# Down projection of chunks 0 and 1 as one Strassen pair, with q, k, v of two chunks in turn and a later exponential

## The chip, the cores and the metric

The kernel runs on one core of a Trainium2 chip. The metric is the device time of one execution in microseconds (us). Before the change it is 777.04 us, the median of three runs (776.59 to 777.09). Times in the text are us from the start of the profiled span unless something else is said.

## The reference

The input `x` has 2048 tokens of 1024 bf16 values. The kernel computes a layer norm, sliding-window attention with a residual, a second layer norm and a bilinear feed-forward part with a residual:

```
h   = x + attention(layernorm(x) @ wqkv) @ wo       # wqkv 1024 x 3072, wo 1024 x 1024
g   = layernorm(h) @ w_gate ;  u = layernorm(h) @ w_up      # 1024 x 3584 each
out = h + (g * u) @ w_down                                  # 3584 x 1024
```

Attention has 32 heads of 32 values. Token s looks at the eight tokens s, s-2, ..., s-14 of its head, with a softmax over the eight logits; positions before the first token are masked.

## The kernel before, in words

**Tiling.** The tokens are cut into four chunks of 512 (`TC`). A product with a weight runs on the tensor array in groups of eight matmuls of 128x128 by 512 columns (`mm_group`, L409), one for each 128 of the 1024 input values. Each group fills one of eight PSUM tiles ("mm"), which another engine has to copy out before it can be used again. For q, k, v there are six weight blocks of 512 columns per chunk and four groups per block (`qkv`, L414). ScalarE copies each group out (`evac_qkv`, L322: a copy of 512 columns, and for k and v two small copies of the 16 columns that the next chunk needs), and SyncE stores it to DRAM.

**Layer norm 1.** Its rows must be transposed before the array can use them. For chunk 3 ScalarE computes sums and squares (`NormOnScalar.sums`, L259) and the four normalized row tiles (`rows`, L277). Each tile of 128 tokens is then transposed by a DMA that SyncE issues (`transpose`, L225) into `lnT`. A q, k, v group reads all four of them.

**Attention.** `attention(c)` (L444) is a generator that mostly emits VectorE work: products of q with shifted k (L451), sums over the head (L453 to L461), the maximum (L466 to L470), an exponential on ScalarE (L471), sums and a reciprocal (L474 to L479), weights times shifted v (L494 to L504). Its operands qD, kD, vD are gathered from DRAM by loads that GpSimd issues (`load_qk` L428, `load_v` L435). The output goes to DRAM (L506) and comes back transposed as four quarters of `oT` (L509), for the output projection.

**Order of the work.** The program is written as one stream of instructions, and each engine runs its part of it in order. `Background` (L37) mixes the generators into the main loops. After each group the main loop calls `bg.step(1.73)`, which adds that time to a credit, times a rate, with a cap of 4.0; while the credit is positive, the next generator that is ready runs until its next `yield`, whose value is taken from the credit. A `yield "later", t` sets the generator aside for t us of the main loop's clock.

The main order is: q, k, v of chunks 0 and 1 (blocks partly in turn); all six blocks of chunk 2 (L765); blocks 0 to 3 of chunk 3; the output projection with layer norm 2 of chunk 0 (`wo_ln2`, L519); blocks 4 and 5 of chunk 3; gate and up of chunk 0 (`ffn1`, L602); `wo_ln2` of chunk 1; the plain down projection of chunk 0 (`ffn2`, L640, 224 matmuls at L646); gate and up of chunk 1; and then the down projection of chunk 1 alone by Strassen's scheme in Winograd's form.

**Strassen.** A product of two-by-two blocks is done with seven block products in place of eight, for additions of blocks on VectorE. Chunk 1's seven products are `dprod` (L805), each 2 x 14 = 28 matmuls, 196 in all, between the output projections of chunks 2 and 3 (`wo_adds`, L846). The operands are f16 and scaled by powers of two. The scales come from sums of absolute values, which ScalarE computes with its activation function (`abs_sum` L585, `abs_sum_down` L590, `abs_sum_h1` L598). Chunks 2 and 3 do gate and up, and then down, as a Strassen pair (`pair_block` L703; the down stage from L1053): there the two chunks are the two rows of blocks.

**Weights.** A list (`stream`, L129 to L157) fixes the order in which SyncE loads weight tiles into seven slots. `retire` frees slots and `pump` (L161) starts the next loads. Normalized rows and the outputs of the absolute sums that nobody reads ("junk") share a pool `ln` of four slots (L101).

Of the kernel before, what the change touches and what calls it, by code (L numbers as in the profile page):

```python
# [36 lines left out]
class Background:  # L37
# [15 lines left out]
    def step(self, us):  # L53
        self.now += us
        self.credit = min(self.credit + us * self.rate, 4.0)
# [23 lines left out]
def kernel(  # L79
# [41 lines left out]

    bg = Background()
# [13 lines left out]
    def stream_wd(c, hf):  # L136
        for b in range(4):
            stream.append((("wd", c, hf, b), wd_v[:, bass.ts(b, 7), bass.ts(hf, 512)], 7))

    NH = NF // 4  # L140
    for c in range(2):
        stream_wo(c)
        if c > 0:
            stream_wd(0, 0)
            stream_wd(0, 1)
        for b in range(7):
            stream.append((("wg", c, b), wg_v[:, :, bass.ts(b, 512)], KO))
            stream.append((("wu", c, b), wu_v[:, :, bass.ts(b, 512)], KO))
    def stream_down(name, e, hf, halves):
        for a in halves:  # L150
            stream.append((("dn", name, a), wd_e[e][:, bass.ts(a, 7), bass.ts(hf, 512)], 7))

    stream_down("21", 1, 0, (0, 1))
    stream_down("11", 0, 0, (0, 1))
    stream_wo(2)
    stream_down("12", 0, 1, (0,))
# [100 lines left out]
    class NormOnScalar(Norm1):  # L257

        def sums(self):  # L259
            room = small.tile([128, 4, 4], F32, tag="nroom", name=f"nroom{self.c}")  # L260
            self.s, self.nm, self.ss, self.nb = (room[:, i, :] for i in range(4))
            junk = lnp.tile([128, D], BF, tag="ln", name=f"njunk{self.c}")
            xs = xtiles[self.c]
            for t in range(4):
                nc.scalar.activation(junk[:], xs[t][:], ACTF.Copy, accum_out=self.s[:, t:t + 1])
                yield "later", GROUP_US
            nc.scalar.activation(self.nm, self.s, ACTF.Copy, scale=-1.0 / D)
            for t in range(4):
                nc.scalar.activation(junk[:], xs[t][:], ACTF.Square, bias=self.nm[:, t:t + 1],
                                     accum_out=self.ss[:, t:t + 1])  # L270
                yield "later", GROUP_US
# [4 lines left out]

        def rows(self):  # L277
            for t in range(4):
                ln = lnp.tile([128, D], BF, tag="ln", name=f"ln{self.c}_{t}")
                nc.scalar.activation(ln[:], xtiles[self.c][t][:], ACTF.Identity, bias=self.nb[:, t:t + 1],  # L280
                                     scale=self.rs4[:, t:t + 1])
                self.lns[t] = ln
                self.transpose(t)
                yield "later", GROUP_US
# [158 lines left out]

    def attention(c):  # L444
        qD, kD = qkv_in["q", c], qkv_in["k", c]
        lg = att.tile([128, W, SUB], F32, tag="lg", name=f"lg{c}")
        for wp in range(W // 2):
# [14 lines left out]
            yield 1.0  # L462
        if c == 0:
            nc.vector.tensor_tensor(lg[0:32, :, 0:16], lg[0:32, :, 0:16], mask[:], ALU.add)
# [5 lines left out]
        nc.vector.tensor_tensor(lg[:], lg[:], mx[:, None, :].to_broadcast((128, W, SUB)), ALU.subtract)  # L470
        nc.scalar.activation(lg[:], lg[:], ACTF.Exp, scale=float(DH) ** -0.5)  # L471
# [38 lines left out]
        oTs[c] = oT  # L510
        while c + 1 < NCH and ("q", c + 1) not in qkv_in:
# [7 lines left out]
    def wo_ln2(c):  # L519
# [8 lines left out]
        for t in range(4):  # L528
            for hf in range(2):
# [12 lines left out]
                bg.spend(0.7)  # L542
                bg.step(GROUP_US)
        norm(3)
        retire(2)
        return lnT, hs
# [35 lines left out]
    scale_gu, scale_d, scale_h = Scale("gu", 56), Scale("d", 56), Scale("h", 56)  # L582
    scale_h1 = Scale("h1", 28)

    def abs_sum(c, b, j):  # L585
        wt = wts["wg" if c == 0 else "wu", c, b]
        junk = lnp.tile([128, 2, 512], BF, tag="ln", name=f"junk{c}_{b}_{j}")
        scale_gu.add(28 * c + 4 * b + j, wt[:, bass.ts(j, 2), :], junk[:])

    def abs_sum_down(hf, b, j):  # L590
        junk = lnp.tile([128, 512], BF, tag="ln", name=f"junkd{hf}_{b}_{j}")
        scale_d.add(28 * hf + 7 * b + j, wts["wd", 0, hf, b][:, j, :], junk[:])
# [5 lines left out]
    def abs_sum_h1(f, ht):  # L598
        junk = lnp.tile([128, TC], BF, tag="ln", name=f"junke{f}")
        scale_h1.add(f, ht[:], junk[:])  # L600

    def ffn1(c, lnT, at={}):  # L602
        hT = []
        for b in range(7):
            if b == 5 and c + 1 < NCH:
                hss[c + 1] = load_x(c + 1, "h", nc.sync)
            for j in range(4):
                pg = psum.tile([128, TC], F32, tag="mm", name=f"pg{c}_{b}_{j}")
                mm_group(pg, wts["wg", c, b], j, lnT)
                gs = t1k.tile([128, TC], BF, tag="t1k", name=f"gs{c}_{b}_{j}")  # L610
                nc.scalar.copy(gs[:], pg[:])  # L611
                bg.step(GROUP_US)
                pu = psum.tile([128, TC], F32, tag="mm", name=f"pu{c}_{b}_{j}")
                mm_group(pu, wts["wu", c, b], j, lnT)
                us = t1k.tile([128, TC], BF, tag="t1k", name=f"us{c}_{b}_{j}")
                nc.scalar.copy(us[:], pu[:])  # L616
                nc.vector.tensor_tensor(gs[:], gs[:], us[:], ALU.mult)  # L617
                abs_sum(c, b, j)
                bg.spend(0.45)
                bg.step(GROUP_US)  # L620
                hT.append(gs)
                if (b, j) in at:
                    at[b, j]()
                f = len(hT) - 3
# [533 lines left out]
```

## Time and profile before

| what | value |
|---|---|
| median of 3 runs | 777.04 us (776.59 to 777.09) |
| profiled execution | 777.01 us, of which the span is 775.2 us |
| tensor array (PE) | 769.3 us busy, 3691 matmuls and transposes |
| VectorE | 605.3 us busy |
| ScalarE | 484.0 us busy |
| GpSimd | 142.1 us busy |
| DMA | 134.38 MB, mean 173 GB/s |
| granted clock of the array | full speed in all 40 slices |

| stage | from (us) | to (us) | matmul groups |
|---|---|---|---|
| plain down projection of chunk 0 | 301.7 | 350.0 | 224 matmuls |
| chunk 1's Strassen, output projections of 2 and 3 | 446.6 | 516.8 | 196 of Strassen and 128 |
| pair of chunks 2 and 3, gate and up | 516.8 | 687.0 | |
| pair of chunks 2 and 3, down | 687.0 | 775.2 | |

How to read a group line of the profile: it names the source line, the engine, the operation, output and inputs, the shape and the count; then the busy time in us with the mean of one in ns, and the idle time of the engine just before these instructions, with what ended most of it. A matmul's duration of 379 ns overlaps with the next one; the pitch of the array is the busy time divided by the count. In a timeline line the first number is the start and the second the duration; an issue on a queue (SPq is SyncE's, ACTq ScalarE's) lasts while the queue hands out the transfer, and a bracket gives how long the engine had been idle and what released it.

### The profile page before, as it was taken

To read this page: it belongs to the slowest core of one execution; us is meant where nothing else is said; L and a number is where in the kernel's file an instruction comes from. 1 tells how busy PE (TensorE), PEld (TensorE's weight loads), DVE (VectorE), ACT (ScalarE), POOL (GpSimd) and SP (SyncE) were. 2 spreads that over 40 slices of the span, in tenths; PEclk is the share of its full clock that TensorE was granted. 3 is DMA by queue.
4 is the path that set the end of the run, shared out by engine and by line. 5 is a ranking of instruction groups with operands and counts; after the bars stand their busy time and mean duration, and the time that the engine had idled before them with its cause. 6 is when DMAs were issued, how large, how long until landed. Compare 5 with 4: busy or idle time off the path is not lost.

```text
span 775.2 us, 10420 instructions
## 1 busy us (share of the span) xinstructions
PE 769.3 (99%) x3691; PEld 353.5 (46%) x3691; DVE 605.3 (78%) x766; ACT 484.0 (62%) x1040; POOL 142.1 (18%) x152
## 2 busy tenths in 40 slices
PE   8999999999999999999999999999999999999998
PEld 6444444444444444444444444444444444444444
DVE  5639999999999989999979859985553444578863
ACT  4639564322866662965777899746677776788240
POOL 0000000200002000011000001008778687600000
PEclk9999999999999999999999999999999999999999
DMA  8998896997947964978445592644332423740001
GB/s 278 265 260 199 157 230 151 299 271 224 310 133 236 308 235 125 288 257 277 142 143 192 182 299 68 157 98 114 109 95 69 109 59 106 240 140 28 0 28 55
DMA packets 183716, 134.38 MB, mean 173 GB/s; under 512 B 81264, under 2 KB 176496, under 8 KB 181616
## 3 DMA queue, kind: packets, MB, share of 16 engines
q1 hardware_dynamic: 176912, 110.12, 50.9%
q0 software_dynamic: 3584, 22.02, 8.9%
q10 hardware_dynamic: 3168, 1.57, 0.8%
q8 instruction: 29, 0.48, 0.3%
q14 instruction: 23, 0.19, 0.1%
HBM read 104.86 MB, written 22.02 MB: 164 GB/s over the span
## 4 chain that ended last, share of the span: by engine, by line
PE 93%; DVE 3%; DMA 2%; ACT 1%; issue 0%; ACTq 0%; DVEq 0%
PE ps L411 20%; PE pg L411 12%; PE pu L411 12%; PE dx L807 6%; PE pz L700 6%; PE acc L646 6%; PE py L700 6%; PE px L700 6%; PE wo L532 4%; PE wo L852 4%; PE pv L700 3%; PE dy L807 3%; PE ex L807 2%; DMA lnT<-lnr 1%; DMA w_qkv<-in_A_wqkv_dram 1%; PE ps L372 1%
## 5 line engine op out<-in xcount | busy, mean ns | idle before, releaser
L411 PE MATMUL ps<-lnT,w_qkv 128*128 128x512 bf16 x736 | 159.5, 379 | 0.0
L411 PEld LDWEIGHTS <-w_qkv 128*128 128x128 bf16 x736 | 71.9, 98 | 86.2
L411 PE MATMUL pu<-lnT,w_wu 128*128 128x512 bf16 x448 | 105.8, 379 | 0.0
L411 PE MATMUL pg<-lnT,w_wg 128*128 128x512 bf16 x448 | 105.8, 379 | 0.0
L324 ACT CAST sg<-ps 128x512 bf16<-128x512 f32 x96 | 55.2, 585 | 52.3 <-PE ps L411 49.2
L451 DVE TENSOR_TENSOR prod<-qD,kD 128x4096 bf16<-128x4096 bf16 x32 | 72.4, 2285 | 12.8 <-DMA kD<-kd 12.7
L494 DVE TENSOR_TENSOR pv<-vD,at 128x4096 bf16<-128x4096 bf16 x32 | 72.5, 2285 | 0.3
L700 PEld LDWEIGHTS <-sw 128*128 128x128 f16 x448 | 43.8, 98 | 53.8 <-issue 1.2
L411 PEld LDWEIGHTS <-w_wu 128*128 128x128 bf16 x448 | 43.8, 98 | 52.9
L411 PEld LDWEIGHTS <-w_wg 128*128 128x128 bf16 x448 | 43.7, 98 | 52.8
L616 ACT CAST us<-pu 128x512 bf16<-128x512 f32 x56 | 33.0, 590 | 43.0 <-PE pu L411 41.8
L700 PE MATMUL px<-lnT,ws 128*128 128x512 bf16 x224 | 55.2, 379 | 0.0
L700 PEld LDWEIGHTS <-ws 128*128 128x128 f16 x336 | 32.9, 98 | 39.7
L506 POOL DMA_DIRECT2D od<-oD x4 | 2.2, 542 | 264.3 <-DVE oD L504 264.3
L646 PE MATMUL acc<-w_wd,gs 128*128 128x512 bf16 x224 | 48.5, 379 | 0.0
L681 POOL TENSOR_TENSOR sw<-ws 128x512 f16<-128x512 f16 x26 | 30.0, 1152 | 85.1 <-PE py L700 77.8
L611 ACT CAST gs<-pg 128x512 bf16<-128x512 f32 x56 | 32.6, 583 | 12.9 <-PE pg L411 10.6
L453 DVE TENSOR_TENSOR prod<-prod 128x4096 bf16<-128x4096 bf16 x16 | 36.6, 2289 | 0.4
L560 ACT ACTIVATE junkd<-w_wd 128x512 bf16<-128x512 bf16 x56 | 34.3, 613 | 0.0
L646 PEld LDWEIGHTS <-gs 128*128 128x128 bf16 x224 | 21.9, 98 | 26.4
L617 DVE TENSOR_TENSOR gs<-gs,us 128x512 bf16<-128x512 bf16 x56 | 23.5, 419 | 12.5 <-ACT us L616 12.5
L185 ACT ACTIVATE rs<-mv,eps 128x1 f32<-128x1 f32 (+1 forms) x21 | 6.2, 297 | 42.0 <-DVE mv L182 36.6
(321 smaller groups left out, 1391.5 us busy)
## 6 DMA issues: line engine op xcount, KB each, us to landing
w_wg<-in_B_w_gate_dram SPq DMA_DIRECT2D x14, 1024.0 KB, 6.7
w_wu<-in_B_w_up_dram SPq DMA_DIRECT2D x14, 1024.0 KB, 5.4
w_wd<-in_B_w_down_dram SPq DMA_DIRECT2D x8, 896.0 KB, 6.2
w_pair<-in_B_w_gate_dram SPq DMA_DIRECT2D x14, 512.0 KB, 4.0
w_pair<-in_B_w_up_dram SPq DMA_DIRECT2D x14, 512.0 KB, 5.2
w_wo<-in_A_wo_dram SPq DMA_DIRECT2D x6, 1024.0 KB, 6.2
w_qkv<-in_A_wqkv_dram SPq DMA_DIRECT2D x5, 1024.0 KB, 11.0
kd<-sg SPq DMA_DIRECT2D x32, 144.0 KB, 3.3
```

Of the source, the lines that this page charges most:

```text
L324: nc.scalar.copy(sg[:, HB:HB + TC], ps[:])
L411: nc.tensor.matmul(ps[:], lhsT=wt[:, ko, bass.ts(j, 128)], rhs=rhs[:, ko, :], start=(ko == 0), stop=(ko == KO - 1))
L451: nc.vector.tensor_tensor(prod[:, j], qD[:], kD[:, :, o:o + SUB], ALU.mult)
L453: nc.vector.tensor_tensor(prod[:, :, 0:16], prod[:, :, 0:16], prod[:, :, 16:32], ALU.add)
L494: nc.vector.tensor_tensor(pv[:, j], vD[:, :, o:o + SUB], at[:, w, None, :].to_broadcast((128, DH, SUB)), ALU.mult)
L532: nc.tensor.matmul(ps[:], lhsT=oTs[c][:, kk, t, :], rhs=wts["wo", c, hf][:, kk, :], start=(kk == 0), stop=(kk == KO - 1))
L560: nc.scalar.activation(junk, src, ACTF.Abs, accum_out=self.l1[:, k:k + 1])
L611: nc.scalar.copy(gs[:], pg[:])
L616: nc.scalar.copy(us[:], pu[:])
L646: nc.tensor.matmul(acc[t][:], lhsT=hT[f][:, bass.ts(t, 128)], rhs=wts["wd", c, hf, b][:, j, :], start=(f == 0), stop=(f == NF - 1))
L700: nc.tensor.matmul(ps[:], lhsT=lhs[:, ko, :], rhs=rhs[:, ko, :], start=(fresh and ko == 0), stop=(ko == 3), skip_group_check=not fresh)
L807: nc.tensor.matmul(ps[:, bass.ds(lo, n)], lhsT=lhs[k][:, bass.ts(q, 128)], rhs=rhs[k][:, bass.ds(lo, n)], start=(fresh and k == 0), stop=( ...
```

## The change

- **Down projection.** Chunks 0 and 1 become one Strassen pair: seven products (`dprod`) of 4 x 14 matmuls, 392 in all, in place of the plain 224 of chunk 0 and the 196 of chunk 1. It stands after gate and up of both chunks, from the first product to the output projection of chunk 3 and four products after it.
- **Chunk 1's g*u** is written to DRAM (`hd1`, 14 stores of 256 KB) and loaded again as the operands a21 and a22 (a22 twice). The rows `h` that the final addition needs are saved to `hsd` and loaded again.
- **Absolute sums.** Those of w_down come from a new generator `abs_down`: 28 loads of 256 KB issued on ScalarE's queue into one weight slot, each followed by a 1024-wide sum on ScalarE, in the q, k, v stage. Those of gate and up are 2048 wide, 28 instead of 56.
- **q, k, v of chunks 2 and 3** run block by block in turn for blocks 0 to 3. The array comes to chunk 3's first group after 441 matmul slots instead of 601.
- **Exponential.** Before it `attention` yields `"later"` (7.0 for chunk 0, else 4.0), so that other instructions of ScalarE are emitted ahead of it. In the order of ScalarE it then stands behind three more q, k, v evacuations and behind the sum number 4 of `abs_down`.
- **Background.** The cap of the credit goes from 4.0 to 8.0, the later rate from 0.98 to 1.0; `attention(c)` waits until chunk c-1 is over.
- **Output projection of chunk 1** moves from behind gate and up of chunk 0 into it, ahead of block 4 (`wo_1`, slot 1113 of the array instead of 1305), and its layer norm goes from VectorE to ScalarE (`Norm2`).

The diff, cut to its core:

```diff
-        self.credit = min(self.credit + us * self.rate, 4.0)
+        self.credit = min(self.credit + us * self.rate, 8.0)
...
     def attention(c):
+        while c and c - 1 not in over:
+            yield "later", 1.0
...
+        yield "later", 7.0 if c == 0 else 4.0
         nc.scalar.activation(lg[:], lg[:], ACTF.Exp, scale=float(DH) ** -0.5)
...
+    def abs_down():
+        ring = wpool.tile([128, KO, 512], BF, tag="w", name="w_ring")
+
+        def rows_of(p):
+            return ring[:, bass.ts(p % 4, 2), :]
+
+        def load(p):
+            nc.scalar.dma_start(rows_of(p), wd_v[:, bass.ts(p % NP, 2), bass.ts(p // NP, 512)])
+
+        for p in range(4):
+            load(p)
+        yield "later", 12.0
+        for p in range(NF):
+            junk = lnp.tile([128, 2, 512], BF, tag="ln", name=f"junkd{p}")
+            scale_d.add(p, rows_of(p), junk[:])
+            if p + 4 < NF:
+                load(p + 4)
+            yield "later", 1.9 * GROUP_US
+        retire()
...
     start_attention(0)
+    sums = abs_down()
+    bg.add(sums, bg.now + 25.0, first=True)
     qkv(1, range(4))
...
-    qkv(2, range(6))
+    for b in range(4):
+        qkv(2, [b])
+        qkv(3, [b], last=True)
+    hss[0] = load_x(0, "h", nc.sync)
+    qkv(2, range(4, 6))
     start_attention(2)
-    hss[0] = load_x(0, "h", nc.sync)
-    qkv(3, range(4), last=True)
     bg.finish(atts[0])
-    bg.rate = 0.98
+    bg.rate = 1.0
     nxt = wo_ln2(0)
     qkv(3, range(4, 6), last=True)
     start_attention(3)
-    lnT2, hs = nxt
-    hT = ffn1(0, lnT2)
-    bg.finish(atts[1])
-    nxt = wo_ln2(1)
-    for hf in range(2):
-        ffn2(0, hf, hT, hs)
-    lnT2, hs = nxt
+    norm2 = []
+
+    def wo_1():
+        bg.finish(sums)
+        bg.finish(atts[1])
+        n = wo_norm(1)
+        norm2.append(n)
+        norm2.append(n.finish())
+        bg.add(norm2[1], bg.now, first=True)
+
+    hT0 = ffn1_first(nxt[0], {4: wo_1})
+    bg.finish(norm2[1])
+    ffn1_second(norm2[0].lnT, {})
...
+    for q in range(4):
+        dprod(xs[q], q, A11, cells_of(b11, NH), True)
...
+    for q in range(4):
+        dprod(xs[q], q, A12, cells_of(b21, NH), False)
+        put(0, q, 0, hs0[q][:, 0:512], xs[q], 1.0, hs0[q][:, 0:512])
...
+    for q in range(4):
         ev = psum.tile([128, TC], F32, tag="mm", name=f"ev{q}")
+        dprod(ev, q, FS1, fcells(b11), True)
...
+    for q in range(4):
+        dprod(ys[q], q, F11, fcells(t2), False)
...
+    for q in range(4):
+        dprod(ys[q], q, F12, fcells(b22), False)
...
+    for q in range(4):
+        dprod(zs[q], q, F11, fcells(b12), False)
...
+    for q in range(4):
+        dprod(zs[q], q, F22, fcells(t4), False)
+        put(1, q, 0, hsr1[:, q, 0:512], zs[q], inv1, hsr1[:, q, 0:512])
```

## Prediction

> **What bounds the kernel now.** I read the page first: busy times, then the chain that ended last, then the cost groups; after that the waits of the array, and the timelines of four queues around the places that the diff moves.
>
> ```profile
> PE 769.3 (99%) x3691; PEld 353.5 (46%) x3691; DVE 605.3 (78%) x766; ACT 484.0 (62%) x1040; POOL 142.1 (18%) x152
> ...
> PE 93%; DVE 3%; DMA 2%; ACT 1%; issue 0%; ACTq 0%; DVEq 0%
> ...
> L646 PE MATMUL acc<-w_wd,gs 128*128 128x512 bf16 x224 | 48.5, 379 | 0.0
> ```
>
> The array (PE) is busy 99% of the span of 775.2 us and carries 93% of the chain; the L646 group has no idle time before it. So a matmul removed is worth its whole slot, and a wait added to the array costs its whole length. One slot: 48.5 us / 224 = 216 ns (the 379 ns of a row is overlapped; the stage from 301.69 to 350.04 gives 215.8). The waits of the array say how closely everything else follows:
>
> ```profile
> PE warm_ps L318 <- DVE warm L304: 1.2, 1, 1.2
> PE pv L700 <- DVE h L812: 0.6, 2, 0.4
> ```
>
> After the start-up the array waits for 0.6 us in all. Every new wait of the array is therefore visible. The place where I expect one is the first use of chunk 3's normalized rows. The four transposes that write them, on SyncE's queue, in the timeline of before:
>
> ```profile
> 84.50 1.26 SPq L229 DMA_TRANSPOSE lnT<-ln  x1
> 85.85 0.52 SPq L337 DMA_DIRECT2D vd<-sg  x1
> 86.47 4.25 SPq L229 DMA_TRANSPOSE lnT<-ln  x1
> 90.80 0.53 SPq L337 DMA_DIRECT2D vd<-sg  x1
> 91.42 11.07 SPq L229 DMA_TRANSPOSE lnT<-ln  x1
> 102.59 0.53 SPq L337 DMA_DIRECT2D vd<-sg  x1
> 103.21 2.85 SPq L229 DMA_TRANSPOSE lnT<-ln  x1
> ```
>
> Issue of the third alone holds the queue for 11.07 us. Asked one at a time, the four land 6.8, 19.3, 16.1 and 7.0 us after issue, at 91.3, 105.8, 107.5 and 110.2. The view of line 229 gives the second of them (first line), that of line 526, the transposes after chunk 0's and 1's output projection, the second line:
>
> ```profile
> DMA to landing us min/median/max: 19.3/19.3/19.3
> ...
> DMA to landing us min/median/max: 3.0/3.1/4.2
> ```
>
> Same instruction, six times slower. What is different shows in GpSimd's timeline, the loads of attention's operands:
>
> ```profile
> 84.30 0.53 POOL L437 DMA_DIRECT2D vD<-vd  x1 [39.85 <-DMA vd<-sg]
> 88.11 0.53 POOL L431 DMA_DIRECT2D qD<-qd  x1 [3.28 <-DVE prod L451]
> 88.63 0.53 POOL L432 DMA_DIRECT2D kD<-kd  x1
> ```
>
> By the DMA view vD lands after 6.1 us, qD after 14.6 and kD after 16.9 (105.5). From 93 to 105 both sides trickle. Before, this hurts nobody: chunk 3's rows are first read at 135.8. Last, ScalarE and the output path of attention(1):
>
> ```profile
> 89.00 1.24 ACT L280 ACTIVATE ln<-x,nroom,rs 128x1024 bf16<-128x1024 bf16 x1
> 97.03 1.06 ACT L471 ACTIVATE lg<-lg 128x1024 f32<-128x1024 f32 x1 [6.79 <-DVE lg L470]
> ...
> 236.17 0.54 POOL L506 DMA_DIRECT2D od<-oD  x1 [62.50 <-DVE oD L504]
> 245.09 3.54 POOL L509 DMA_DIRECT2D oT<-od  x4 [8.39 <-PE pg L411]
> ```
>
> ScalarE is in order: chunk 0's exponential held it for 6.79 us, unharmed. VectorE is 96 to 97% busy from 52 to 236 us, so what delays it there arrives at 236.17, and oT of chunk 1 some 12.6 us later at the earliest (245.09 + 3.7 = 248.8 for its first quarter, 253.3 for the second).
>
> **What the Trainium skill says.** "DMA: Bandwidth & Descriptors", section "Issuing engines are not separate DMA queues": what SyncE, ScalarE and GpSimd start runs on the same 16 DMA engines and interleaves. Same page, "Queues, rings and completion order": each DMA engine takes turns between queues, one packet at a time. The trace agrees in kind: transposes (256 B pieces) beside the 8 to 9 KB pieces of qD and kD take 16 to 19 us, alone 3.1. It doesn't explain why both trickle. "PSUM — Partial Sum Buffer", section "PSUM: the matmul accumulator": 8 banks, and a 512-column f32 result fills one. So the array can run 8 groups of 8 matmuls (8 x 1.73 = 13.8 us) past an evacuation that is stuck; the 7.8 us gap of evacuations from 89 to 98 stalled nothing, which fits.
>
> **The change part by part.** The profiled execution is 777.01 us, 775.2 of it the span; the median of the runs is 777.04, so I sum against 777.01.
>
> *Down projection.* Before: 224 plain matmuls (L646) and 196 of chunk 1's own Strassen. After: seven products x 4 x 14 = 392. Gate, up, q, k, v and output projection keep their counts. 28 x 215.8 ns = **-6.04 us**, to 770.97. All of it is on the path.
>
> *Interleaving q, k, v of chunks 2 and 3.* No matmul more or less, but chunk 3's first group stands behind 441 matmul slots instead of 601. Time of a slot: 6.1 + 0.2158 x position (this gives 163.4 for the first output projection, the trace 163.5). So lnT of chunk 3 is needed at **101.3** instead of 135.8. All four transposes are needed, as a group reads 512 tokens. On before's landings that is 110.2 - 101.3 = 8.9 us of waiting.
>
> Do they land earlier or later now? Ahead of the first of these rows ScalarE gets six DMA issues and two absolute sums of w_down that it did not have (`abs_down`): 6 x 0.5 (ScalarE's issues at L296: 0.48 to 0.53) + 2 x 1.05 (pitch of its 1024-wide sums at L265) = 5.1, less some 1.75 idle that before had between 78 and 83. The row starts at 83.2 + 3.4 = 86.6, its transpose at 87.9, the second at 89.8, the third after one more sum and issue at 93.3. The vD load waits for v stores that ScalarE delays as much: 87.9. The qD and kD loads wait for VectorE's last product, which does not move: 88.1. So transposes and three loads (3.3 MB) start together, and the ring of w_down adds 0.25 MB each 3.3 us. Also the `ln` pool has four slots, which sums and rows now share: the fourth row waits until the first transpose has landed, and the sums numbered 4, 5 and 7 until the second, third and fourth have. Best case, the smaller backlog behind the third lets all land by 103; worst, even the first waits for the kD load and the fourth lands at 115. I take 110.3, as before, since the kD load that they end with ends at about the same time: **+9.0 us**, bounds +1.7 and +13.7.
>
> *Exponential later.* It stands behind sum 4 in ScalarE's order. Behind it on ScalarE: the evacuations of the q, k, v groups, for which the array waits once eight are open, and the v stores; VectorE waits for it with everything of attention(0). Sum 4 waits for the second transpose, 105.8 before; so the exponential runs at about 107 instead of 97.03, and VectorE is 10 us later. Without the block it would be only the added load: ScalarE was done at 90.2; nine issues (4.5), five sums (5.25) and three evacuations that now stand ahead (2.3), less the 1.75 idle, give 100.5, 3.5 later. The array stands still meanwhile for the same cause, so the evacuations cost nothing more.
>
> *Output projection of chunk 1 earlier.* From slot 1305 (287.7) to 1113 (246.3). oT's first quarter lands at 248.8 + 10 = 258.8; the array comes at 246.3 + 9.0 = 255.3: 3.5 us. The second quarter (263.3) is needed two groups later, 258.8 + 3.5 = 262.3, another 1.0, less what VectorE catches up in its 3 to 4% idle before 236 (up to 1.5). **+3.0 us**, bounds 0 and +7. If the first wait is absent, this one is 2.5 + 3.5 = 6.0 at most: the two replace each other in part.
>
> *Absolute sums.* 56 x (613 + 187 ns) leave ScalarE's 35.3 busy us of the plain down stage; 28 x 1.05 and 28 issues x 0.5 come before it, and gate and up sums are as many elements in half the instructions. Beyond the delay costed above the eight banks hide this: 0; with the cover gone, one sum and one issue at the array, 1.6.
>
> *Stage of the pair.* h of chunk 1 goes out in 14 stores of 256 KB and comes back: 3.5 MB + 3 MB with other loads from 398 to about 418 at the 300 to 350 GB/s of the best slices; needed at 420. VectorE's list (f16 conversions at 1.07 per 3584, sums at 1.93, 14 h additions at 0.60, attention(3)'s rest) just fits between its products: slack 0.2 to 3.6 us by my addition. After a 12 us delay of the array VectorE and the loads have more. 0, bounds 0 and +3. First pair block: 0.6 before, 0.4 to 2.3 after: 0.
>
> Sum: 777.01 - 6.04 + 9.0 + 3.0 = **783.0**.
>
> **Rivals.** *The transposes come in time* (other sign): for it, 3.1 us each when alone, and SyncE's issue order leaves them no other obstacle; against it, all of 93 to 105. It decides at a landing of 101.3 + about 4: below that the sum is under 777. With landing at 103 (1.7) and a wait of 2 for chunk 1's oT: 770.97 + 3.7 = 774.7. *Half of it*: landing at 105, 3.7, then 2.3 for oT: 777.0, no change. *ScalarE blocked twice*: the first transpose is caught as well, lands at 104, so the fourth row and its transpose come after it, landing at 113, exponential at 111: 11.7 + 5.8 gives 788.5. For it: issue at 87.9 together with the vD load, which alone held the first one of before until 89.5.
>
> **Chances.** Forecast 0.44, blocked twice 0.24, half 0.12, in time 0.20. A measurement of this kernel tells about 0.2% from no change: under 775.5 is faster, above 778.6 slower. Faster 0.2, same 0.12, slower 0.68. The range goes from 772.5 (part of the in-time case left out below) to 791 (blocked twice with 2.5 in the pair's stage); the likeliest case alone is 779 to 787.
>
> **What would show it.** Right: a wait of the array of 7 to 11 us at chunk 3's first q group near 101 to 111 for the transposes; ScalarE idle before sums 4 or 5; the exponential past 104; a second wait at chunk 1's output projection; 392 down matmuls at 216 ns. Wrong: transposes landing within 5 us of issue, or a wait over 3 us in the stage of the pair, which I put at nothing.

## The result and the profile after

The changed kernel takes 796.77 us (median of 4 runs, 794.09 to 798.30) against 777.07 before (4 runs). The ratio is 1.0251, with a 95% interval of 1.0218 to 1.0285: 19.7 us slower. One run each of two experiments below (e11 and e12) was in a slower state than the others of its kernel and is left out of the median. The profiled execution took 798.30 us, of which 795.9 are the span.

The page after, its busy times, the clock granted to the array in 40 slices, and the chain that ended last:

```profile
PE 769.4 (97%) x3663; PEld 352.0 (44%) x3663; DVE 608.0 (76%) x722; ACT 509.4 (64%) x981; POOL 141.9 (18%) x152
...
PEclk9999979999999999999998999999999999999999
...
PE 45%; DVE 35%; ACT 9%; issue 6%; DMA 4%; SPq 1%; ACTq 0%; DVEq 0%
```

The 28 matmuls are gone (3691 to 3663), yet the array is as long busy as before, at 97% of a longer span. Slices in which the clock is below full are new. And VectorE is now 35% of the chain, where it was 3%. The waits of the array in the changed kernel (who waited, for which engine's or DMA's result; total us, how many, longest):

```profile
PE ps L430 <- DMA lnT<-ln: 10.9, 1, 10.9
PE ey L641 <- DVE rowbd L636: 6.2, 1, 6.2
PE pg L430 <- ACT sg L346: 2.5, 1, 2.5
PE warm_ps L337 <- DVE warm L323: 1.2, 1, 1.2
PE ey L641 <- DVE rowbh L636: 0.8, 1, 0.8
PE ps L430 <- DVE h L600: 0.7, 1, 0.7
```

The waits are not the whole loss. After each long one the array runs at half clock for some microseconds. This table by stretches of the changed kernel shows it; its columns are the stretch, its length, the array's busy time (and matmuls), the granted clock, the DMA share and GB/s:

```profile
101.00:112.10 11.10, 0.17 (x2) 0.68 1.11 267
112.10:118.00 5.90, 5.90 (x21) 0.73 0.69 168
```

From 112.1 to 118 the array is busy all the time but starts 21 matmuls, where 5.9 / 0.2158 = 27 would fit. I sum the loss from the starts of the matmuls instead: every interval between two starts counts with what it exceeds 215.8 ns.

| place (us) | loss | of it waiting |
|---|---|---|
| 101 to 115, chunk 3's first q group | 12.7 | 10.9 |
| 189 to 190, chunk 0's output projection | 0.8 | 0.7 |
| 204 to 211, first gate groups | 4.3 | 2.5 |
| 422 to 433, first products of the pair | 8.9 | 6.9 |
| 540, first block of chunks 2 and 3 | 0.4 | 0.2 |

Together 27.1. The profiled execution of before (777.01) - 6.04 - 1.0 (its own loss at its first pair block) + 27.1 = 797.1; measured 798.3. The end of the span and what lies around it account for 0.7 of the remaining 1.2.

**The loss at 101.** The transposes of chunk 3's rows on SyncE's queue after, and the loads on GpSimd's:

```profile
92.81 1.64 SPq L231 DMA_TRANSPOSE lnT<-ln  x1
...
95.18 9.61 SPq L231 DMA_TRANSPOSE lnT<-ln  x1
...
105.51 1.28 SPq L231 DMA_TRANSPOSE lnT<-ln  x1
...
107.50 1.28 SPq L231 DMA_TRANSPOSE lnT<-ln  x1
```

```profile
91.85 0.53 POOL L456 DMA_DIRECT2D vD<-vd  x1 [45.51 <-DMA vd<-sg]
92.37 0.53 POOL L450 DMA_DIRECT2D qD<-qd  x1
92.89 0.53 POOL L451 DMA_DIRECT2D kD<-kd  x1
```

The four land 12.7, 11.7, 2.7 and 4.5 us after issue, the last at 112.0. The first two stand beside the three loads, which land at 97.9, 100.7 and 104.4; the last two do not. They start 8 us later than before, because ScalarE is later:

```profile
70.73 2.56 ACTq L667 DMA_DIRECT2D w_ring<-in_B_w_down_dram  x4
73.34 1.06 ACT L273 ACTIVATE njunk<-x 128x1024 bf16<-128x1024 bf16 x1 [7.21 <-DMA kd<-sg]
...
105.49 1.24 ACT L295 ACTIVATE ln<-x,nroom,rs 128x1024 bf16<-128x1024 bf16 x1 [6.49 <-DMA lnT<-ln]
...
112.47 1.06 ACT L498 ACTIVATE lg<-lg 128x1024 f32<-128x1024 f32 x1
```

The ring loads are those of w_down into the weight slot `w_ring`. ScalarE ends an evacuation at 66.1 and issues the first of them at 70.7. The profile puts the whole gap of 7.2 us down to stores of k. In the trace each of the four issues waits for a completion count (a semaphore that tells of a DMA's landing) which one of SyncE's stores uses too: the first goes out at 70.73, when a store of q has landed (70.71), the others when stores of k have (71.50, 72.23, 72.90). Then ScalarE stands 6.5 us before the fourth row, for the landing of the first transpose, since both share a slot of the `ln` pool. The exponential runs at 112.5 instead of 97.0, and VectorE waits 13.4 us for it (1.1 before).

**The losses from 189 to 211.** VectorE is now late with the additions of chunk 0's output projection, and ScalarE stands in order behind its statistics:

```profile
193.64 0.29 ACT L187 ACTIVATE rs<-mv,eps 128x1 f32<-128x1 f32 x1 [14.29 <-DVE mv L184]
```

In before the same wait was there:

```profile
176.94 0.29 ACT L185 ACTIVATE rs<-mv,eps 128x1 f32<-128x1 f32 x1 [12.65 <-DVE mv L182]
```

12.65 us and no wait of the array, within the 13.8 us that the prediction counted for the eight banks; 14.29 us is over it.

**The loss at 422.** The array waits for a cast of one column, `rowbd`. VectorE's timeline ahead of it:

```profile
425.22 2.29 DVE L521 TENSOR_TENSOR pv<-vD,at 128x4096 bf16<-128x4096 bf16 x1
427.43 0.68 DVE L733 TENSOR_TENSOR ring<-ring 128x1024 bf16<-128x1024 bf16 x1
428.03 0.18 DVE L635 TENSOR_REDUCE rowd<-l1d 128x1 f32<-128x28 f32 x1
428.24 0.16 DVE L636 CAST rowbd<-rowd 128x1 bf16<-128x1 f32 x1
```

`rowd` and `rowbd` are the row sums: they add up, row by row, the absolute values that set the scales. The array then makes the total of them (L641), and with it VectorE makes the seeds (`seed`: the first products times the scales, on which later products add). The row sums take 0.3 us. They stand behind attention(3), whose eight large operations (2.29 us each) fill VectorE from 408 to 427.

### The profile page after: what moved, and what is told of

It reads as the page before. It is cut to its first block, busy times and chain, and to the rows that moved or that the text cites. A ratio compares the mean times of both kernels' runs of the same rounds, so it can differ in the third digit from the quotient of the medians.

```text
span 795.9 us, 10296 instructions
## 1 busy us (share of the span) xinstructions
PE 769.4 (97%) x3663; PEld 352.0 (44%) x3663; DVE 608.0 (76%) x722; ACT 509.4 (64%) x981; POOL 141.9 (18%) x152
## 4 chain that ended last, share of the span: by engine, by line
PE 45%; DVE 35%; ACT 9%; issue 6%; DMA 4%; SPq 1%; ACTq 0%; DVEq 0%
DVE pv L521 6%; PE dx L924 6%; PE py L805 6%; PE pz L805 6%; PE px L805 6%; DVE prod L476 6%; PE ps L430 5%; PE pv L805 3%; PE ey L924 3%; PE dy L924 3%; DVE oD L531 3%; DVE pv L529 3%; PE ex L924 2%; DVE prod L478 2%; PE wo L1018 2%
## 5 line engine op out<-in xcount | busy, mean ns | idle before, releaser
L430 PE MATMUL ps<-lnT,w_qkv 128*128 128x512 bf16 x736 | 161.4, 382 | 11.7 <-DMA lnT<-ln 10.9
L476 DVE TENSOR_TENSOR prod<-qD,kD 128x4096 bf16<-128x4096 bf16 x32 | 72.1, 2285 | 13.8 <-DMA kD<-kd 13.8
L430 PE MATMUL pg<-lnT,w_wg 128*128 128x512 bf16 x224 | 54.3, 387 | 2.5 <-ACT sg L346 2.5
L805 PE MATMUL px<-lnT,ws 128*128 128x512 bf16 x224 | 55.2, 379 | 0.0
L430 PE MATMUL pu<-lnT,w_wu 128*128 128x512 bf16 x224 | 53.2, 381 | 0.0
L430 PE MATMUL pwg<-lnT,w_wg 128*128 128x512 bf16 x224 | 52.9, 379 | 0.0
L430 PE MATMUL pwu<-lnT,w_wu 128*128 128x512 bf16 x224 | 52.9, 379 | 0.0
L924 PEld LDWEIGHTS <-gs 128*128 128x128 f16 (+1 forms) x280 | 27.8, 99 | 34.0 <-issue 1.9
L822 ACT COPY py<-px 128x512 f32<-128x512 f32 x28 | 16.0, 570 | 28.6 <-PE px L805 28.6
L631 ACT ACTIVATE ring<-ring 128x1024 bf16<-128x1024 bf16 x14 | 14.8, 1057 | 27.2 <-DVE ring L733 24.2
L787 POOL TENSOR_TENSOR sw<-sw,ws 128x512 f16<-128x512 f16 x26 | 30.0, 1152 | 2.0
L789 POOL TENSOR_TENSOR sw<-ws,sw 128x512 f16<-128x512 f16 x26 | 30.2, 1160 | 0.0
```

Of the source, the lines that this page charges most:

```text
L430: nc.tensor.matmul(ps[:], lhsT=wt[:, ko, bass.ts(j, 128)], rhs=rhs[:, ko, :], start=(ko == 0), stop=(ko == KO - 1))
L476: nc.vector.tensor_tensor(prod[:, j], qD[:], kD[:, :, o:o + SUB], ALU.mult)
L787: eng.tensor_tensor(sw[:, i, 1], sw[:, i, 0], a11, ALU.subtract)
L789: eng.tensor_tensor(sw[:, i, 3], a12, sw[:, i, 1], ALU.subtract)
L805: nc.tensor.matmul(ps[:], lhsT=lhs[:, ko, :], rhs=rhs[:, ko, :], start=(fresh and ko == 0), stop=(ko == 3), skip_group_check=not fresh)
L924: nc.tensor.matmul(ps[:, bass.ds(lo, n)], lhsT=lhs[k][:, bass.ts(q, 128)], rhs=rhs[k][:, bass.ds(lo, n)], start=(fresh and k == 0), stop=( ...
```

## The experiments

After the result I had two theories. *Array*: the wait for the transposes at 101 is a loss of its own, the others are separate. *VectorE*: the late exponential puts VectorE 15 us behind, and the array would meet that delay anyway. Later two more are on VectorE in the stage of the pair: *order* (what the array needs stands behind work that could wait) and *amount* (there is more work than time). Each result below is a median with the 95% interval of its ratio to the kernel before (776.9 to 777.2 in all series). "Loss" is the sum from the starts of matmuls in the profiled run.

### Which part makes the loss at 101

`e1_no_turn`, on the changed kernel:

```diff
-    for b in range(4):
-        qkv(2, [b])
-        qkv(3, [b], last=True)
-    hss[0] = load_x(0, "h", nc.sync)
-    qkv(2, range(4, 6))
+    qkv(2, range(6))
     start_attention(2)
+    hss[0] = load_x(0, "h", nc.sync)
+    qkv(3, range(4), last=True)
```

> The changed kernel with q, k, v of chunks 2 and 3 not in turn (chunk 2 whole, then chunk 3), all else kept. Theory 'array' (the wait of 10.9 us for chunk 3's transposes is a loss of its own, with 1.7 us of half clock after it): about 12.7 us go, to 784. Theory 'VectorE' (the exponential at 112.5 instead of 97.0 puts VectorE 15 us late, and the array would only meet that delay later, at chunk 0's output projection and behind ScalarE): the wait at 101 goes, but waits near 164 to 205 grow by about as much; 792 to 797.

Measured: 798.02 us (1.0256 to 1.0299). The wait at 101 stays although nobody needs chunk 3's rows there, and it has another name:

```profile
PE ps L430 <- ACT halo L348: 9.8, 1, 9.8
...
PE wo L598 <- DMA w_wo<-in_A_wo_dram: 4.9, 1, 4.9
```

ScalarE stands 7.9 us for the first transpose, evacuates nothing, and the banks fill. So two things end at the same place: the array needs the transposes itself, and ScalarE needs them to empty the banks. Both theories missed this. The second line is weights that come late: w_wo is issued at 160.5 and 173.9 here, at 125.1 and 136.0 in the changed kernel. The likely reason, not tested, is that without turns the blocks of q, k, v hold their slots longer while the ring keeps one.

`e2_in_place`, on the changed kernel:

```diff
-            junk = lnp.tile([128, 2, 512], BF, tag="ln", name=f"junkd{p}")
-            scale_d.add(p, rows_of(p), junk[:])
+            scale_d.add(p, rows_of(p), rows_of(p))
```

> The changed kernel, but the unread output of the sums of w_down is written over its own input, so that the ln pool no longer makes ScalarE wait for the transposes (6.5 us before chunk 3's fourth row). Theory 'VectorE': the exponential comes at about 106, VectorE is 9 us late instead of 15, less than the array's 12.7; the losses near 190 and 204 (0.8 and 4.3) go and that near 422 (8.9) shrinks: 784 to 791. Theory 'array': the transposes still land near 112, nothing else changes: 796.

Measured: 794.71 us (1.0196 to 1.0260), the profiled run 791.97. The exponential came at 106.1, as expected. The array still waits 7.8 us for transposes (loss 10.3), the losses from 189 to 211 are gone, and the one near 422 is 10.7.

This says less than it seems to, for two reasons. First, the edit took ScalarE's wait away in one place, and the next ring load brought it back: its issue shares a completion count with the first transpose, which landed at 101.37.

```profile
66.16 2.07 ACTq L667 DMA_DIRECT2D w_ring<-in_B_w_down_dram  x4
...
101.44 0.38 ACTq L667 DMA_DIRECT2D w_ring<-in_B_w_down_dram  x1
102.16 0.58 ACT L343 CAST sg<-ps 128x512 bf16<-128x512 f32 x1 [6.04 <-DMA lnT<-ln]
```

So ScalarE stood 6.0 us for the transposes where it had stood 6.5. Second, this run was early before the edit could act, as ScalarE's instructions differ only from 80 us on: the first ring load went out at 66.2 instead of 70.7, chunk 3's first row ran at 86.5 instead of 91.5, and VectorE began attention at 50.5 instead of 55.2. The profiled runs of e3 and e15 were as early (66.0, 66.1), those of e1 and e5 as late as the changed kernel's (71.3, 70.9). So about 5 of the 6.4 us by which the exponential came earlier are not the edit's, and the two medians are not clear of each other's noise. What can be kept: with VectorE 6 us less late, whatever the cause, the losses from 189 to 211 are gone, as 'VectorE' has it, and the one near 422 is not.

`e3_both` joins the two edits.

> Both edits. Theory 'VectorE': the array is on time and VectorE 9 us late, so waits of 5 to 8 us near 164 to 205, and what stays of the one near 422: 780 to 788, and less than either edit's result. Theory 'array': as without turns alone, 784.

Measured: 794.53 us (1.0216 to 1.0261): loss 4.2 at 101, 7.9 at chunk 0's output projection (5.5 of it weights), 9.9 near 420. That is no better than e2 alone: late weights stand where the wait for the turns stood.

`e4_before_turn` makes the reverse test, the kernel **before** with the turns alone (the edit of e1 backwards).

> The kernel before with one part of the change alone: q, k, v of chunks 2 and 3 in turn. Theory 'array': chunk 3's transposes land near 110 while the array comes at 101, 8.9 us and some 1.5 of half clock: 785 to 788. Theory 'VectorE': the exponential stays at 97 and VectorE on time, so nothing is added to that wait and part of it is given back as no later wait exists: also 785 to 788. A result under 780 would say that the transposes land sooner when nothing else is in their way.

Measured: 787.59 us (1.0115 to 1.0195). One long wait is added:

```profile
PE ps L411 <- DMA lnT<-ln: 8.1, 1, 8.1
```

With half clock the loss is 10.1. The forecast's 8.9 for this part stands.

### Why the transposes are slow

`e6_before_turn_late_loads` adds to e4 a wait on GpSimd's queue. A tiny operation there reads the softmax weights, so the loads behind it can't start before these exist:

```diff
-        prefetch_qk(c + 1)
         while ("v", c) not in qkv_in:
...
+        nc.gpsimd.tensor_tensor(mask[:, 0, 0:1], at[0:32, 0, 0:1], at[0:32, 1, 0:1], ALU.add)
         yield 1.2
         oD = att.tile(
```

> The kernel before with q, k, v of chunks 2 and 3 in turn (787.6, its array waiting 8.1 us for transposes) and GpSimd's loads of the next chunk's q and k held back until VectorE has written the weights of the softmax (about 102 for chunk 0; they are needed at 136). If these loads are what starves the transposes, chunk 3's transposes land by about 98, the wait at 101 is gone and the time is 776 to 779. If the transposes are slow for another cause, they land near 109 as before: 786 to 789.

Measured: 777.25 us (0.9995 to 1.0012). The wait is gone. The transposes are issued in the same order, but the third one's issue takes 1.27 us where it took 11.64 in e4 (11.07 in before):

```profile
86.33 4.19 SPq L229 DMA_TRANSPOSE lnT<-ln  x1
...
91.24 1.27 SPq L229 DMA_TRANSPOSE lnT<-ln  x1
...
93.23 1.27 SPq L229 DMA_TRANSPOSE lnT<-ln  x1
```

They land 3.1 to 6.8 us after issue; in e4 it was 5.4 to 19.9. The q and k loads gain as well (8.4 and 10.7 us, in e4 15.4 and 17.6). That the two kinds of transfer hold each other up is shown. Why is not.

`e15_late_loads` makes the same edit on the changed kernel alone.

> The changed kernel with one edit: GpSimd's loads of the next chunk's q and k held back until the softmax weights are written. If these loads are what holds up chunk 3's transposes here too, ScalarE's wait of 6.5 us before the fourth row shrinks to 1 or 2, the exponential comes near 106, the transposes land near 104, and the wait of 10.9 falls to 2 to 4; the losses near 190 to 211 go with it: 780 to 786. If ScalarE's own lateness (7.2 us before its first ring load) decides, the wait at 101 stays over 7: 790 to 796.

Measured: 793.76 us (1.0156 to 1.0239), 789.9 in the profiled run, the fastest of the four. The last transpose lands at 104.4 and ScalarE stands 2.3 us before the fourth row, about as expected. The wait at 101 is 3.2 us, and it is for ScalarE, not for transposes; loss 5.3, then 2.4 near 195 and 11.4 near 415. The total is not as expected, since the last loss grew. This run too had the early ring load (66.1 us), so not all of the gain at 101 is the edit's; that holding the loads frees the transposes rests on e4 against e6.

`e7_ring_on_sync` is e2 with the ring loads issued by SyncE:

```diff
-            nc.scalar.dma_start(rows_of(p), wd_v[:, bass.ts(p % NP, 2), bass.ts(p // NP, 512)])
+            nc.sync.dma_start(rows_of(p), wd_v[:, bass.ts(p % NP, 2), bass.ts(p // NP, 512)])
```

> The changed kernel with the unread output of the w_down sums in place (794.7 by itself) and the 28 loads of w_down's ring issued by SyncE in place of ScalarE. In the changed kernel ScalarE stood 7.2 us from 66 to 73 before its first ring load, until stores of k had landed. If that wait is what puts the rows of chunk 3 and the exponential late, the exponential comes at 97 to 100 instead of 106, the transposes are issued some 6 us sooner but still land with the q and k loads near 104 to 109: a wait of 3 to 8 at 101; 785 to 792. If the wait was only a bookkeeping of order that another wait replaces, the exponential stays at 105 and the time at 793 to 796.

Measured: 787.28 us (1.0113 to 1.0176); the profiled run, 793.02, is the slowest of the four. The exponential comes at 95.9 (106.1 in e2), so taking the issues off ScalarE was worth 10 us to VectorE: the 6.0 us that ScalarE stood at its issue for a transpose are gone, and the first row runs 3.0 us earlier. The second transpose's issue now takes 17.6 us beside the loads, and the array waits 11.8. The transposes land no sooner (the last at 113.1), though the first is issued 8 us earlier than in the changed kernel.

### What is left when all that is mended

`e9_three` has the three edits: in place, ring on SyncE, late loads. `e8_all` has also the totals of the sums one product later:

```diff
-        if q == 1:
+        if q == 2:
             scale_d.total(ys[2])
...
-            seed(0)
-            seed(1)
             pull(1)
+    seed(0)
+    seed(1)
     seed(2)
```

> The changed kernel with all four: sums in place, ring loads on SyncE, q and k loads held back, totals one product later. If the three causes found (transposes behind the loads, ScalarE standing, row sums late) are all that eats the 28 matmuls, the time is near 771 to 774, under both kernels. If there is a further bound (VectorE in the stage of the pair), 775 to 782.

> The changed kernel with three edits: w_down's sums in place, their loads on SyncE, q and k loads held back; the totals at their place in the change. Nothing is lost before 400 then, as in the run with all four; the wait for VectorE's row sums stays. If the later totals only moved that wait (into the products that wait for the seeds), this run is as slow or a little faster, 783 to 787; if they helped, it is slower, 790.

`e5_late_total` makes that last edit on the changed kernel alone.

> The changed kernel with the totals of the absolute sums one product (6.0 us of the array) later, and all four seeds behind the fourth product. If the loss of 8.9 us near 422 is VectorE's queue being late with the row sums (they stood 12 us behind, after attention(3) and the last products of g and u), 6 us of later need take away most of the 6.2 + 0.8 of waiting and the half clock with it: 788 to 791. If VectorE is behind in all of the stage and only meets the array elsewhere, the loss moves to the products after it: 795 to 798.

Measured: e8 787.31 us (1.0113 to 1.0153), e9 785.41 (1.0070 to 1.0130), e5 801.51 (1.0295 to 1.0337). Later totals don't help: in e5 and e8 the wait for the row sums falls to some 4 us, and a new one of 3.5 to 4.0 for the seeds follows it. In e9 nothing is lost at 101. The loss near 408 is 9.1. e9 lost 4.4 near 190 as well and e8 0.6. As the two kernels differ only after 400, this is chance: VectorE began attention at 53.95 in e9 and at 50.21 in e8, as the first k load landed. (Of the runs below, e11 and e16 began at about 54 and lost 4.5 and 2.9 there, e13, e14 and e17 at about 51 and lost nothing.) Shown by these: the pair's stage has a loss of its own, about 9 us.

`e10_exp_early` is e9 with the exponential back at its former place (the line `yield "later", 7.0 if c == 0 else 4.0` taken out).

> The run with three edits, and the exponential emitted at its former place, right after the maximum is subtracted. In the run with all four VectorE stood 4.8 and 2.9 us for the exponentials of chunks 2 and 3, behind sums on ScalarE. Theory 'VectorE is full from 310 to 430, and each us that it idles before is missing at the row sums': 5 to 8 us off the three edits' time. Theory 'the lateness comes from the order alone, attention(3) ahead of the row sums': no difference, since VectorE's list is the same: within 2 us.

Measured: 797.78 us (1.0227 to 1.0290). Both expectations fell. ScalarE now stands 7.9 us for the exponential ahead of chunk 3's third and fourth rows. Their transposes are issued at 99.0 and 102.0. The third still lands after 2.8 us; the fourth goes out together with the held loads and takes 19.9:

```profile
102.35 0.57 POOL L450 DMA_DIRECT2D qD<-qd  x1
102.92 0.53 POOL L451 DMA_DIRECT2D kD<-kd  x1
```

```profile
PE ps L430 <- DMA lnT<-ln: 21.0, 1, 21.0
```

So in this kernel the later exponential lets the rows pass. The turns as such don't need it: in e6, whose ScalarE has no sums of w_down to do at that time, the exponential stands at its former place, the rows are out before it, and nothing is lost. With the array 21 us late nothing is lost near 420: VectorE has reached the row sums by then.

`e12_exp_sums` is e10 with part of w_gate's sums moved to chunk 1:

```diff
-                if j % 2:
+                if j % 2 and b < 4:
                     abs_sum("wg", b, j // 2, junk[:])
...
                             abs_sum("wu", b, j // 2, junk)
+                            if b >= 4:
+                                abs_sum("wg", b, j // 2, junk, 1)
```

> The run with three edits and the early exponential, and the sums of w_gate's last three blocks moved from chunk 0's gate and up to chunk 1's, where ScalarE has room. In the changed kernel ScalarE had no idle time from 283 to 320 (norm of chunk 1 beside sums and evacuations), and VectorE waited there for its g and u tiles (4.0 us). Theory 'VectorE is full': 3 to 4 us off the run with the early exponential, 775 to 779. Theory 'order alone': no difference.

Measured: 791.99 us (1.0157 to 1.0277), with 16.7 us of the same wait. It tells nothing on its question.

### Order or amount of VectorE's work

`e13_hold_v` is e9 with attention(3) held before its weighted sum of v:

```diff
+        while c == 3 and not state.get("go"):
+            yield "later", 1.0
         vD = qkv_in["v", c]
...
     seed(3)
+    state["go"] = True
...
-        for _ in range(n):
+        for _ in range(2 * n):
             next(atts[3], None)
```

> The run with three edits (785.4), and attention(3) held before its weighted sum of v until the four seeds are emitted, then drawn twice as fast. Theory 'order': seven operations of 2.3 us no longer stand ahead of the row sums, the wait of 6.3 + 0.8 us and the half clock go: 9 us off, 775 to 778. Theory 'amount': VectorE meets the array again at chunk 3's output projection or in the products that wait for sums of blocks: 781 to 786.

`e14_hold_less_v` also leaves out half of the weighted sum for chunk 3 (`range(W // 2 if c < 3 else W // 4)`); `e11_less_v` leaves it out on e9 without the hold.

> The same with half of chunk 3's weighted sum of v left out, so that attention's result is wrong for that chunk. If an amount of VectorE's work is left over after the order is mended, it goes here: 772 to 775, and 2 us or more under the run with v held. If not, both are equal within 1 us.

> The run with three edits, with half of the weighted sum of v left out for chunk 3 (4 of its 8 window positions), so that attention's result is wrong for that chunk, and about 20 us of VectorE's work in and after the stage of the pair's start are gone. Theory 'VectorE is full': the wait for the row sums and what follows shrinks by most of its length, 772 to 777. Theory 'order alone': the four large operations ahead of the row sums are still emitted there, so the wait stays: 782 to 787.

`e16_hold_sums` is e13 with the sums of e12.

> The run with v held, and the sums of w_gate's last three blocks moved to chunk 1's gate and up. VectorE idles 9 us between 275 and 300 behind ScalarE in the run with all four. If that idle is what VectorE lacks later, 2 to 4 us off the run with v held; if the order was all, no difference within 1 us.

`e17_hold_less` holds attention(3) after the first of its four pairs instead.

> The run with three edits, attention(3) held after the first of its four pairs until the seeds are emitted, then drawn twice as fast. Theory 'order': the row sums come by 408, VectorE has no idle time of more than 3 us, and nothing is lost later: 774 to 778. Theory 'amount': the output of attention(3) is no earlier than in the run with three edits (issued near 475), and the array, now 9 us earlier, waits for it or for VectorE's sums of blocks: 779 to 786.

Measured: e13 799.76 us (1.0252 to 1.0325), e14 780.01 (1.0016 to 1.0039), e11 783.43 (1.0043 to 1.0088), e16 805.79 (1.0309 to 1.0393), e17 794.82 (1.0225 to 1.0276). Holding mends the wait for the row sums (in e13 they are made at 403.5, in e9 at 414.6) and loses more later. The waits of e13, and then of e14:

```profile
PE wo L1020 <- DMA oT<-od: 8.7, 1, 8.7
PE ey L925 <- DVE gs L1091: 7.0, 2, 4.3
PE ey L643 <- DVE totd L645: 1.6, 1, 1.6
```

```profile
PE ps L430 <- ACT sg L343: 2.2, 1, 2.2
PE wo L1020 <- DVE h L1022: 1.5, 3, 0.6
```

The work left out in e14 is 8 operations of 2.29 us, 18.3 us. The time falls by 19.7, not quite to the 772 to 775 expected. In e11 the same work is out, but the eight operations ahead of the row sums stay, and the loss there stays (8.4). By itself e11 speaks for 'order': less work behind the row sums doesn't mend them.

VectorE by stretches; the columns after the length are busy times and counts of the array, its weight loads, VectorE, ScalarE and GpSimd, then clock, DMA share and GB/s. First e9, then e13, e14 and e17:

```profile
390.00:408.00 18.00, 17.95 (x85) 8.12 (x84) 17.16 (x14) 11.70 (x19) 2.29 (x1) 1.00 0.45 152
408.00:433.00 25.00, 17.67 (x74) 7.58 (x75) 23.59 (x31) 10.52 (x11) 0.00 (x0) 0.86 0.85 290
433.00:470.00 37.00, 36.95 (x173) 16.74 (x172) 36.83 (x49) 28.22 (x37) 0.57 (x1) 1.00 0.49 171
```

```profile
390.00:408.00 18.00, 16.26 (x75) 7.25 (x76) 4.50 (x20) 15.39 (x25) 0.00 (x0) 1.00 0.82 269
408.00:433.00 25.00, 24.90 (x115) 11.29 (x116) 20.04 (x18) 16.05 (x10) 2.28 (x1) 1.00 0.68 232
433.00:470.00 37.00, 32.33 (x147) 14.13 (x145) 36.97 (x44) 18.93 (x31) 0.00 (x0) 1.00 0.44 157
```

```profile
390.00:408.00 18.00, 17.90 (x83) 8.14 (x84) 4.29 (x16) 15.39 (x25) 0.00 (x0) 1.00 0.80 262
408.00:433.00 25.00, 24.90 (x116) 11.30 (x117) 20.31 (x23) 15.97 (x10) 2.28 (x1) 1.00 0.68 231
```

```profile
433.00:470.00 37.00, 33.98 (x155) 15.05 (x155) 36.93 (x42) 21.84 (x36) 0.00 (x0) 1.00 0.50 174
```

From 433 to 470 VectorE is busy 36.8 of 37 us or more in e9, e13 and e17, whatever stands where: in this stretch it has no time to give. But the hold wastes VectorE ahead of it. From 390 to 433 VectorE stands idle for 2.2 us in e9, for 18.5 in e13, 18.4 in e14 and 15.8 in e17, most of it for tiles of ScalarE (in e16 still more, so that run tells nothing on its question). The longer waits of the array in the stage follow: 7.1 us in e9, 19.4 in e13, 14.8 in e17. And the 18.3 us left out in e14 are about what its hold wastes.

So these runs show that VectorE's time in this stage is spent to the last few microseconds, and that the array pays for much of what is wasted there. They don't settle order against amount, since no run has the row sums early and VectorE busy. An estimate from them, if the array pays for all of it: e13's waits less the 16.3 us that it wastes beyond e9 are 3.1, e17's less 13.6 are 1.2. Another: in e9 the first quarter of `oT` for chunk 3 lands at 481.2 and is needed at 486.2; an array 9.1 us earlier would wait 4.1 for it. So an order without waste might wait 1 to 4 us where e9 waits 7.1: the larger part would be order, the rest amount. Such an order was not run. None of the kernels that do the whole work is faster than the one before.

## Why the prediction was wrong

The sign was right and the size was not: 783.0 was forecast, in a range to 791, and 796.8 came. By its own steps:

- **Down projection, -6.04.** Right: 28 matmuls fewer at the same pitch.
- **Interleaving, +9.0.** The mechanism was right. The wait was 10.9 here and 8.1 in e4, and e6 shows that the loads of attention cause it. What the sum left out is half clock: 1.8 here, 5.6 over the three long losses (12.7 + 4.3 + 8.9 lost, 10.9 + 2.5 + 6.9 waited). That the bare wait came so near to the forecast for the whole kernel is partly luck: the transposes started 5 us later than the forecast had them, and the first of them was caught, which the forecast gave to a rival.
- **ScalarE's lateness, 5.1 - 1.75.** A term was missing. I costed a DMA issue at 0.5 us and at no waiting. In this run the first ring load stood 4.6 us before its issue, behind stores of q and k whose completion counts it shares, so chunk 3's first row came at 91.5, not at 86.6. In the profiled runs of e2, e3 and e15, in which these stores landed earlier, it came at 86.5 to 86.9, as forecast. So the sum was right for a run in which no issue stands.
- **Exponential at 107.** It came at 112.5, as in the rival 'blocked twice' (111): the first transpose was caught as well and landed at 105.5. That rival had 788.5.
- **Output projection of chunk 1, +3.0.** Wrong place. No wait arose there. VectorE's delay met the array at chunk 0's output projection and behind it instead, 5.1 us, through ScalarE standing 14.3 us for VectorE. Before, the same wait stood at 12.65 and I had room of 13.8 in the text; I didn't hold the two against each other.
- **Stage of the pair, 0, bounds 0 and +3.** This is the step that failed: "VectorE's list ... just fits between its products". The array waited 6.9 us there for the row sums and lost 8.9 in all, and between 7.8 and some 12.6 in the runs where ScalarE or the loads were mended (e2, e3, e7, e8, e9, e15). I had followed the list from the stage's start, with only a "rest" of attention(3) in it. But VectorE carries attention of all four chunks, 2.3 us a large operation. In before the plain down projection of chunk 0 gave it room: 48.4 us of the array in which VectorE was busy 47.25 (the third busy time), 41 us of it with attention. And attention(3) was over when chunk 1's Strassen began:

```profile
301.70:350.10 48.40, 48.40 (x226) 21.90 (x225) 47.25 (x34) 35.30 (x116) 3.22 (x5) 1.00 0.78 241
...
437.61 2.28 DVE L504 TENSOR_TENSOR oD<-oD,pv 128x4096 bf16<-128x4096 bf16 x1
...
446.60 6.21 PE L807 MATMUL ex<-w_dn,gs 128*128 128x512 f16 x28
```

The changed kernel has no plain stage, and its pair begins that much earlier, behind 1949 matmuls and transposes instead of 2174, with attention(3) still on:

```profile
416.10 6.21 PE L924 MATMUL ex<-w_dn,gs 128*128 128x512 bf16 x28
...
479.10 2.29 DVE L531 TENSOR_TENSOR oD<-oD,pv 128x4096 bf16<-128x4096 bf16 x1
```

So the list of the pair and the end of attention(3) meet, and the row sums stand behind eight large operations of it. e13 shows that the place in the order makes the wait at the row sums, and e9, e13 and e17 that VectorE then has no time left up to 470. "After a 12 us delay of the array VectorE and the loads have more" was wrong too: VectorE had been delayed by 15, 12.3 of it at the exponential and 3.2 by a later start of attention (55.2 against 52.0).

770.97 - 1.0 + 27.1 = 797.1, against 798.3 in the profiled execution. To the forecast of 783.0 that is 3.7 more at chunk 3's rows, 2.1 at the output projections, 8.9 in the stage of the pair, and 0.6 less at the first pair block (0.4 instead of 1.0).

What stays open: why transposes and loads slow each other; why the first k load of attention lands anywhere between 50 and 56 us in the runs of the changed kernels, and with it the stores before ScalarE's ring loads; and how much of the pair's 9 us an order with early row sums and no idle VectorE would save. Moving VectorE's work to GpSimd wasn't tried.

## What to carry to other kernels

A cut of the bottleneck engine's work is worth its time only if the stage that loses it was not the room in which another engine caught up: ask what each engine does in that stage, and by when it must be done. When work is moved earlier, trace what it waits for on every in-order queue, with the shared slots and completion counts of its DMAs; here the same late transposes held the array directly and once more through ScalarE. Moving a late operation in a full engine's order can move the wait; and a test that holds work back or leaves it out tells order from amount only if the engine idles no more than before. Before a gain is put down to an edit, look whether the profiled run was ahead already where the edit can't act yet.

## What the runs showed of the hardware

Waits of the array brought half clock. The record of the changed kernel grants 0.5 for 10.24, 3.41 and 6.83 us at its three longest waits (10.9, 2.5 and 6.2), which with the short wait behind the last cost 5.6 us beside the waiting. Over all the runs every wait of 3.1 us or more came with such a record. Of those of 2.4 to 2.5 us four did (in the changed kernel, e3, e9 and e11) and two did not (e5 and e16), and the 2.2 us in e14 did not.

DMA transposes issued with attention's q and k loads, or well before these ended, landed after 11.7 to 22.8 us (changed kernel, e7); issued in the loads' last 4 us after 5.4 to 7.0 (before, e4, e7); beside the v load alone after 5.0 to 12.1 (e9, e8); with none of these loads under way after 2.7 to 5.7 (changed kernel, e2). The loads are slower as well (q and k 15.4 and 17.6 us in e4, 8.4 and 10.7 held back in e6).

An issue on ScalarE's queue can hold ScalarE until a DMA of SyncE has landed, where both use one completion count: 4.6 us behind stores in the changed kernel, 6.0 us behind a transpose in e2.
